# Strassen's seven block products in the first product of an MLP, on 256 columns, with w1's combinations made once and read back

## The chip, the core and the metric

The kernel runs on one core of a Trainium2 chip. The metric is the time of one execution on the device in microseconds. Five engines work side by side, each on its own queue in order: TensorE (PE; its weight loads are listed apart as PEld), VectorE (DVE), ScalarE (ACT), GpSimd (POOL) and SyncE (SP), which here only issues DMA transfers.

## What is computed

Two layers, each a linear attention and an MLP, both behind a layer norm and added to their input. Tokens S = 2048, width D = 448, 16 heads of 28, hidden width F = 1792; all in fp32.

```python
phi = lambda t: where(t > 0, t + 1, exp(t)) + 1e-6
q, k, v = heads(layernorm(x) @ wqkv)
pq, pk = phi(q), phi(k)
kv, z = einsum("bhsd,bhse->bhde", pk, v), pk.sum(s)
x = x + ((pq @ kv) / (pq @ z + 1e-6)) @ wo
h = gelu(layernorm(x) @ w1 + b1)
x = x + h @ w2 + b2
```

## The kernel before

The order of the work is written out by hand: every engine takes its instructions in the order in which the Python code issues them. fp32 accuracy is reached with fp32r products: an operand is split into a high half (a cast on ACT, "hi" or "h") and a low half (a subtraction, "lo" or "l"), and three products hi x hi, hi x lo, lo x hi are added in PSUM. The width 448 is three chunks of 128 and one of 64; the 64 rows stand twice in the fourth chunk, once with their low half, so that chunk takes two products and not three. One 128-row output with all of D takes 11 products.

A layer has two parts. `phase1` (line 733) walks over 16 tiles of 128 tokens: layer norm (statistics on DVE; the power -1/2 on POOL, line 216), the turn of the tile (DVE turns 32 x 32 squares, a transfer to DRAM and four back put them in place: `store_sq`, `spread`), splits, then k, phi(k), the running sum G of phi(k) x xn, and q. The lists `STEPS` and, after the last tile, `ORDER` (line 667) set the order; a token is one step of one tile. `ORDER` also makes the first block of four tiles ready for the MLP: `la`, `lb` (layer norm), `tu`, `st`, `sp`, `sa` (turn, store, spread) and `x0` to `x3` (the split of each tile into XH and XL).

In the first half of layer 0, the token `bg` calls `background`, which loads w1 and w2 piece by piece and splits them: a cast on ACT, a subtraction on POOL (lines 419 to 431). w1 then stays in SBUF as w1h, w1l, w1x, w2 as w2h, w2l.

The MLP walks over four blocks of 512 tokens, and in each over 14 slices of 128 hidden units. `mlp1` (line 1001) makes one slice: eleven products of 512 columns into a bank hp of PSUM, gelu on ACT into g, a cast on ACT into gh, a subtraction on DVE into gl. `mlp2` (line 1020) adds the slice to four token tiles: twelve products of 448 columns. The loop (line 1207) issues `mlp1(i + 1)` ahead of `mlp2(i)`, so TensorE has a slice's products in hand while ACT and DVE make the next gh and gl. Between the two stands `behind` (line 1097): by the tables `PLAN_0` (for block 1, while block 0 runs), `PLAN_1` and `PLAN`, with `LATER` for the second half of each, it makes the next block's attention output and its layer norm. Its tokens: `z` (POOL) and `p` (DVE: the denominator, the scaling, the turn), `sq`, `lq` (store, spread), `q` (the split), `o` (eleven products of 448 columns on TensorE, then the sum and the statistics on DVE), `n` (norm and turn), `sx`, `lx`, `x` (the split), `ld`, `g` (loads). In the last block of layer 0 the first tiles of layer 1 are prepared instead.

PSUM has eight banks: four of tag "acc" (the four token tiles of `mlp2`), two of tag "h" (hp), two of tag "m" (the output products `op`).

Of the kernel before, what the change touches and what calls it, by code (L numbers as in the profile page):

```python
# [22 lines left out]
def linear_attn_mlp_kernel(  # L23
# [22 lines left out]
    NG = D // G  # L46
    TL = D - 64
# [149 lines left out]
    w1h = wts.tile([128, 3, F], F32R, name="w1h")  # L197
    w1l = wts.tile([128, 3, F], F32R, name="w1l")
    w1x = wts.tile([128, F], F32R, name="w1x")
# [33 lines left out]
    class Block:  # L233
        def __init__(self, key):
            at = APART if key[0] == "a" else 0
            self.rows = key[0] == "m"
            self.hi = work.tile([128, 2048], F32R, name="XH", tag="XH", bufs=2)
            self.lo = work.tile([128, 2112], F32R, name="XL", tag="XL", bufs=2)[:, at:at + 2048]

        def pieces(self, t):  # L240

            if self.rows:
                return tuple(x.rearrange("p (c t n) -> p t c n", c=4, t=4)[:, t] for x in (self.hi, self.lo))
            s = slice(t * 512, (t + 1) * 512)
            return self.hi[:, s], self.lo[:, s]

        def moving(self, x, c):

            return x[:, c * 512:(c + 1) * 512]

        def still(self, x, t, c):

            return x[:, (t * 4 + c) * 128:(t * 4 + c + 1) * 128]

# [70 lines left out]
    def half_square(name, j):  # L325

        if j >= 2:
            return t512("AB"[j - 2], 2, name)
# [34 lines left out]
    def proj(name, key, j, o=None, cs=range(4), at=(3, 6, 9, 11)):  # L363
# [3 lines left out]
        if len(cs) == 4:  # L367
            w = [wkq[name, c] for c in range(3)]
            his = [(b.still(b.hi, j, c), p) for c in range(3) for p in w[c]] + [(b.still(b.hi, j, 3), wkq[name, 3])]
            los = [(b.still(b.lo, j, c), w[c][0]) for c in range(3)] + [(b.still(b.lo, j, 3), wkq[name, 3])]  # L370
# [3 lines left out]
        for c in cs:  # L374
            if c < 3:
                hi, lo = wkq[name, c]
                pe.matmul(o, b.still(b.hi, j, c), hi, start=(c == 0), stop=False)
                pe.matmul(o, b.still(b.hi, j, c), lo, start=False, stop=False)
                pe.matmul(o, b.still(b.lo, j, c), hi, start=False, stop=False)
            else:  # L380
                pe.matmul(o, b.still(b.hi, j, 3), wkq[name, 3], start=False, stop=False)
                pe.matmul(o, b.still(b.lo, j, 3), wkq[name, 3], start=False, stop=True)
# [12 lines left out]
    def bg_pieces():  # L395
        n = 0
        both = []

        def stage():
            nonlocal n  # L400
            n += 1
            if n <= LATE:
                k = (n - 1) // 2
                if k % 2 == 0 or k > 5:
                    return t512("xn", 2, "stg")[:, :D]

                if n % 2:
                    both.append(half("stg"))
                return both[-1][:, n % 2 * 512:][:, :D]
            return t448(f"W{5 + n % 2}", 1, "stg")  # L410

        for fc in range(4):
            sl = slice(fc * D, (fc + 1) * D)
            for c in range(4):
                s = stage_piece(w1[:, sl], c, sp, stage())

                def go(c=c, s=s, sl=sl):
                    if c < 3:
                        act.copy(w1h[:, c, sl], s)
                        pool.tensor_tensor(w1l[:, c, sl], s, f(w1h[:, c, sl]), op=OP.subtract)  # L420
                    else:
                        act.copy(w1x[:, sl], s)
                        pool.tensor_tensor(w1x[64:128, sl], s[64:128], f(w1x[64:128, sl]), op=OP.subtract)
                yield go
        for i in range(NF):
            s = stage()
            sp.dma_start(s, w2[i * 128:(i + 1) * 128, :])

            def go(i=i, s=s):
                act.copy(w2h[:, i], s)  # L430
                pool.tensor_tensor(w2l[:, i], s, f(w2h[:, i]), op=OP.subtract)
            yield go

    bg = bg_pieces()
    bg_wait = []

    def background(n, m=NF):

        for g in bg_wait[:m]:
            bg_wait.pop(0)()  # L440
        for _ in range(n):
            g = next(bg, None)
            if g is not None:
                bg_wait.append(g)
# [47 lines left out]
    def stage_s(l, t):  # L492
        xn = xns.pop((l, t))
        h = t512("A", 2, "xnh", F32R)
        lo = t512("B", 2, "xnl", F32R, APART)
# [81 lines left out]
    def product(name, t, c, p):  # L577
# [8 lines left out]
        pe.matmul(o, b.still(b.lo if p == "l" else b.hi, t, c), w, start=(n == 0), stop=(n == 11))  # L586
# [57 lines left out]
    def stage_g(l, t, acc, mid=lambda: None):  # L644
# [618 lines left out]
```

## Time and profile before

| what | value |
|---|---|
| median of 3 runs | 864.53 us (864.36 to 864.55) |
| profiled execution, whole | 864.72 us |
| its span, first to last instruction | 863.0 us |
| instructions | 11715 |
| TensorE's granted clock | 0.999 of full speed |
| DMA | 97.89 MB, mean 113 GB/s |

In the profile, busy time is given by engine and share of the span; matmuls overlap each other, so the steps from start to start tell what one costs and not its own duration. A group's row names line, engine, operation, output and inputs, the shape, the count, then busy us and mean ns of one, then how long the engine stood idle before these instructions and what ended that. Idle time of an engine that nobody waits for costs nothing.

### The profile page before, as it was taken

The page shows a single profiled execution, that of the slowest core. Times are in us where ns is not written, and L with a number is a line of the kernel's source. Part 1 is how long each engine was busy: PE and PEld are TensorE (multiplying, and loading weights), DVE is VectorE, ACT ScalarE, POOL GpSimd, SP SyncE. Part 2 cuts the span into 40 slices and gives each one's busy share as a digit, 9 for nine tenths or more (in the row PEclk, how much of TensorE's full clock was granted, in tenths as well). Part 3 has the DMA queues.
Part 4 walks back from the last instruction along what each step waited for, and adds up shares of the span by engine and source line. Part 5 has one row for each costly group of instructions (what it writes and reads, how often), then busy time and mean ns, then how long its engine had stood idle before and what let it go on. Part 6 is the DMA issues. An engine that isn't in the chain of part 4 may idle for free.

```text
span 863.0 us, 11715 instructions
## 1 busy us (share of the span) xinstructions
PE 857.2 (99%) x4155; PEld 768.1 (89%) x4155; DVE 493.0 (57%) x962; ACT 352.8 (41%) x635; POOL 211.6 (25%) x244
## 2 busy tenths in 40 slices
PE   9999999999999999999999999999999999999998
PEld 8999988888888888888899998988888888888887
DVE  7888586559456443236477876764664383533112
ACT  7676655323323322333356565633232233233231
POOL 3576612235013012012222343120310140140000
PEclk9999999999999999999999999999999999999999
DMA  5485647633313402051146442462332423111001
GB/s 171 150 270 180 206 108 217 191 113 121 123 61 123 140 0 98 1 182 49 49 150 188 164 130 96 146 204 81 123 113 78 140 74 111 49 49 43 1 1 43
DMA packets 68681, 97.89 MB, mean 113 GB/s; under 512 B 9488, under 2 KB 62864, under 8 KB 68624
## 3 DMA queue, kind: packets, MB, share of 16 engines
q1 hardware_dynamic: 67872, 96.76, 35.0%
q8 instruction: 32, 0.52, 0.3%
q10 hardware_dynamic: 752, 0.41, 0.2%
q14 instruction: 25, 0.20, 0.1%
HBM read 57.74 MB, written 36.18 MB: 109 GB/s over the span
## 4 chain that ended last, share of the span: by engine, by line
PE 90%; DVE 4%; DMA 3%; issue 1%; ACT 1%; POOL 1%; SPq 0%; DVEq 0%; ACTq 0%; POOLq 0%
PE hp L1011 32%; PE y L1041 10%; PE y L1040 10%; PE y L1042 10%; PE psq L372 5%; PE G L658 5%; PE psk L372 5%; PE op L949 2%; PE op L948 2%; PE op L950 2%; DMA sp<-sq_a 1%; PE op L938 1%; PE op L937 1%; PE op L939 1%; PE kvp L824 1%
## 5 line engine op out<-in xcount | busy, mean ns | idle before, releaser
L1017 DVE TENSOR_TENSOR gl<-g,gh 128x512 fp32r<-128x512 f32 x112 | 83.2, 743 | 293.0 <-ACT gh L1016 293.0
L1013 ACT ACTIVATE g<-hp,b1s 128x512 f32<-128x512 f32 x112 | 77.1, 689 | 400.8 <-PE hp L1011 400.8
L1041 PE MATMUL y<-w2l,gh 128*128 128x448 f32 x447 | 163.6, 366 | 0.0
L1040 PE MATMUL y<-w2h,gh 128*128 128x448 f32 x447 | 162.0, 362 | 0.0
L1042 PE MATMUL y<-w2h,gl 128*128 128x448 f32 x447 | 160.0, 358 | 0.0
L1011 PE MATMUL hp<-XH,w1h 128*128 128x512 f32 x336 | 130.7, 389 | 0.0
L1011 PE MATMUL hp<-XH,w1l 128*128 128x512 f32 x336 | 130.7, 389 | 0.0
L1011 PE MATMUL hp<-XL,w1h 128*128 128x512 f32 x336 | 130.1, 389 | 0.0
L216 POOL TENSOR_TENSOR brs<-bve,mhalf 128x1 f32<-128x1 f32 x55 | 34.2, 622 | 258.5 <-DVE bve L215 250.8
L1040 PEld LDWEIGHTS y<-w2h,gh 128*128 128x128 f32 x447 | 83.7, 187 | 9.4
L1041 PEld LDWEIGHTS y<-w2l,gh 128*128 128x128 f32 x447 | 83.9, 188 | 7.0
L1042 PEld LDWEIGHTS y<-w2h,gl 128*128 128x128 f32 x447 | 84.0, 188 | 5.0
L1011 PEld LDWEIGHTS hp<-XL,w1h 128*128 128x128 f32 x336 | 63.1, 188 | 13.1
L1011 PEld LDWEIGHTS hp<-XH,w1h 128*128 128x128 f32 x336 | 63.0, 187 | 10.7
L1011 PEld LDWEIGHTS hp<-XH,w1l 128*128 128x128 f32 x336 | 63.1, 188 | 9.9
L1016 ACT CAST gh<-g 128x512 fp32r<-128x512 f32 x112 | 69.6, 621 | 3.6
L372 PE MATMUL psk<-wk,XH 128*128 128x448 f32 x210 | 61.8, 364 | 0.0
L372 PE MATMUL psq<-wq,XH 128*128 128x448 f32 x196 | 57.0, 365 | 0.0
L497 POOL TENSOR_TENSOR xnl<-x,xnh 128x384 fp32r<-128x384 f32 x32 | 35.0, 1094 | 73.5 <-ACT xnh L496 60.3
L355 DVE TENSOR_TENSOR XL<-sp,XH 128x512 fp32r<-128x512 f32 x58 | 47.2, 825 | 5.7 <-ACT XH L354 5.7
L883 POOL TENSOR_TENSOR pz<-pq,zb 128x448 f32<-128x448 f32 x24 | 28.2, 1174 | 89.9 <-DVE dn L894 61.8
L658 PE MATMUL G<-kh,xnh 128*128 128x448 f32 x128 | 46.7, 367 | 0.0
(194 smaller groups left out, 1500.2 us busy)
## 6 DMA issues: line engine op xcount, KB each, us to landing
x<-in_A_x_dram SPq DMA_DIRECT2D x32, 224.0 KB, 3.9
pq_d<-eq SPq DMA_DIRECT2D x32, 224.0 KB, 2.5
pq<-pq_d SPq DMA_DIRECT2D x32, 224.0 KB, 3.6
x<-x_d SPq DMA_DIRECT2D x32, 224.0 KB, 3.9
sq_a<-sq SPq DMA_DIRECT2D x13, 512.0 KB, 2.9
sp<-sq_a SPq DMA_DIRECT2D x52, 128.0 KB, 2.9
sq_q<-sq SPq DMA_DIRECT2D x12, 512.0 KB, 2.6
sp<-sq_q SPq DMA_DIRECT2D x48, 128.0 KB, 2.8
```

What stands on the lines that cost most here:

```text
L216: pool.tensor_tensor(rs, ve, mhalf, op=OP.pow)
L355: eng.tensor_tensor(lo.rearrange("p c (i n) -> p c i n", n=32), x, f(h), op=OP.subtract)
L372: pe.matmul(o, x, p, start=(i == 0), stop=(i == 10))
L497: pool.tensor_tensor(lo[:, :TL], xn[:, :TL], f(h[:, :TL]), op=OP.subtract)
L658: pe.matmul(acc[c], w, k, start=first and c not in others[0], stop=last and c not in others[1])
L1011: pe.matmul(hp, w, r, start=(k == 0), stop=(k == len(made) - 1))
L1013: act.activation(g, hp, AF.Gelu_apprx_tanh, bias=b1s[:, i:i + 1])
L1016: act.copy(gh, g)
L1017: dve.tensor_sub(gl, g, f(gh))
L1040: pe.matmul(acc[j], gh[:, s], w2h[:, i], start=first, stop=False)
L1041: pe.matmul(acc[j], gh[:, s], w2l[:, i], start=False, stop=False)
L1042: pe.matmul(acc[j], gl[:, s], w2h[:, i], start=False, stop=stop)
```

## The change

The slices of hidden units are taken in pairs p (256 columns of w1, NP = 7 pairs), the tokens of a block in two halves of 256, the width in two halves of two chunks. The pair's product is then a product of 2 x 2 blocks, and is made with seven block products in place of eight (Winograd's form of Strassen's method). With A the tokens and B the pair of w1:

```python
SUMS = {"S1": ("A21", "A22", OP.add), "S2": ("S1", "A11", OP.subtract),
        "S3": ("A11", "A21", OP.subtract), "S4": ("A12", "S2", OP.subtract)}
PRODUCTS = {1: ("a", 0, "A11"), 5: ("a", 4, "S1"), 6: ("a", 8, "S2"), 2: ("b", 0, "A12"),
            7: ("b", 3, "S3"), 3: ("b", 7, "S4"), 4: ("b", 10, "A22")}
```

Products 1, 5, 6, 7 take six matmuls and 2, 3, 4 take five, 39 in all, each of 256 columns, where two slices took 22 of 512. In the whole kernel 2184 matmuls of 256 columns stand for 1232 of 512; the products of `mlp2`, now `quarter`, are as many as before.

*The tokens.* `token_sum` (tokens `c1` to `c4`) makes S1 to S4 on POOL, `token_piece` (`x0` to `x6`) splits A11, S1, S2, A12, S3, S4, A22: seven splits a block for four. In the first block of a layer the sums are halves of 256, eight of them, c1 c3 c2 c4; S2 needs S1, S4 needs S2.

*w1.* w1h, w1l and w1x are gone. `made_pair` makes a pair's combinations: four loads, five POOL sums of 256 columns, two transfers that swap the last chunk's halves, then casts on ACT and subtractions on POOL into two tiles of 12 and 13 x 128 columns, which are stored to DRAM; nine POOL operations of 256 and five of 128 a pair. `bg` takes a quarter of that at a time: twenty in `phase1` of layer 0 (`BG = [0] + [1, 1, 2] * 5`), eight in `ORDER`. In the MLP two pairs are in SBUF; `fetch` reads the next ones back, five of seven in each block after the first two pairs, since blocks go through the pairs in turned order. w2's splits move into layer 0's first block.

*The order in a pair.* X is a bank of tag "h", y and z are the halves of a bank of tag "m". `before` is the pair before, whose `mlp2` products are made in four quarters:

```diff
+            if 1 not in c.done:
+                c.product(1)
+            c.keep_1()
+            c.product(5)
+            c.keep_5()
+            before.rest()
+            q[0]()
+            beside(l, b, 2 * k, tr)
+            c.product(6)
+            c.keep_2()
+            fetch(held_a, fetch_a, n)
+            if 2 not in c.done:
+                c.product(2)
+            c.c11()
+            q[1]()
+            c.product(7)
+            c.c22()
+            q[2]()
+            q[3]()
+            beside(l, b, 2 * k + 1, tr)
+        c.product(3)
+        c.product(4)
+        c.c12()
...
+        def c11(self):
+            dve.tensor_tensor(self.z(), self.s1, self.z(), op=OP.add)
+            self.gelu(11, self.z())
+            self.high(11)
+            self.low(11)
...
+        def c22(self):
+            dve.tensor_tensor(self.s5, self.x(), self.s5, op=OP.add)
+            self.gelu(22, self.s5)
+            self.high(22)
+            self.low(22)
...
+        def c12(self):
+            dve.tensor_tensor(self.y(), self.s2, self.y(), op=OP.add)
...
+        def rest(self):
+            self.gelu(21, self.x())
+            self.gelu(12, self.y())
+            self.high(12)
+            self.high(21)
+            self.low(12)
+            self.low(21)
```

`keep_1`, `keep_5`, `keep_2` copy a half bank on ACT (s1, s5, s2) before the next product is added to it. `gelu` and `high` are on ACT, `low` on DVE, each 256 columns wide. A product that writes a bank waits for what last read the bank, either half of it: product 5 of a layer's first pair, the opening pair, waits for the gelu of c11, product 7 for the copy s2, product 4 for the sum of c22. The opening pair has no `before`: it makes products 1, 2, 5, 6, then products 1 of the next pair, 7, 2 of the next, 3, 4, and the last pair of a layer has its quarters in `last_step`.

*The tables.* The second half of each plan has `c` tokens and other places for `x`:

```diff
-        "x0 p0 z1",
-        "x1 p1 sq0 z2",
-        "x2 p2 z3 lq0",
-        "x3 p3 sq1",
-        "",
-        "lq1",
+        "p0 z1",
+        "c1 c3 p1 sq0 z2",
+        "x0 p2 z3 lq0",
+        "c2 x1 p3 sq1",
+        "c4 x2 x3",
+        "x4 x5 lq1",
```

The first place is DVE's queue in layer 0's first block, around the second pair. Before, from the second slice's low half to the third's (gl; dn, rd, pq0_4, sq are token p of block 1's first tile):

```order
L1017 TENSOR_TENSOR gl_1796<-g_1793,gh_1795 128x512
L894 TENSOR_REDUCE dn_1799<-pz_1736 128x16
L896 TENSOR_TENSOR dn_1799<-dn_1799,dc_1349 128x16
L898 RECIPROCAL rd_1802<-dn_1799 128x16
L905 SCALAR_TENSOR_TENSOR pq0_4_1706<-pq0_4_1706,rd_1802 128x448
L308 STREAM_TRANSPOSE sq_1805<-pq0_4_1706 128x3x4x32
L309 STREAM_TRANSPOSE sq_1805<-pq0_4_1706 128x4x32
L1017 TENSOR_TENSOR gl_1837<-g_1834,gh_1836 128x512
```

Now, from the opening pair's last sum (c12, into hy_2045) to the second pair's c22 (s5_2154; token p is of block 1's third tile):

```order
L1170 TENSOR_TENSOR hy_2045<-s2_2087,hy_2045 128x256
L1154 TENSOR_TENSOR gl_2161<-g_2158,gh_2160 128x256
L1154 TENSOR_TENSOR gl_2161<-g_2156,gh_2160 128x256
L936 TENSOR_REDUCE dn_2180<-pz_2129 128x16
L938 TENSOR_TENSOR dn_2180<-dn_2180,dc_1514 128x16
L940 RECIPROCAL rd_2183<-dn_2180 128x16
L947 SCALAR_TENSOR_TENSOR pq0_6_1977<-pq0_6_1977,rd_2183 128x448
L305 STREAM_TRANSPOSE sq_2186<-pq0_6_1977 128x3x4x32
L306 STREAM_TRANSPOSE sq_2186<-pq0_6_1977 128x4x32
L1158 TENSOR_TENSOR hy_2109<-s1_2146,hy_2109 128x256
L1154 TENSOR_TENSOR gl_2212<-g_2209,gh_2211 128x256
L1164 TENSOR_TENSOR s5_2154<-hx_2091,s5_2154 128x256
```

Before, one subtraction stood between two tokens. Now the token stands between the lows of one pair and the sums of the next, and after each sum comes the low whose gelu and cast on ACT start from that sum.

The second place is ACT's queue at the end of layer 0's attention part. Before, from the split of the first block's tiles (XH) to the first gelu (g; eq is phi(q)):

```order
L354 CAST XH_1674<-sp_1575 128x4x128 x2
L610 ACTIVATE eq_1672<-eq_1672 128x448
L354 CAST XH_1674<-sp_1645 128x4x128
L354 CAST XH_1674<-sp_1654 128x4x128
L610 ACTIVATE eq_1693<-eq_1693 128x448
L598 ACTIVATE eq_1730<-psq_1718 128x448
L599 ACTIVATE eq_1730<-eq_1730 128x448
L205 ACT_TABLE_LOAD
L205 ACTIVATE none_108<-tiny_119 128x1
L1013 ACTIVATE g_1750<-hp_1738,b1s_127 128x512
```

Now, from the split of S1 to the opening pair's first copy, s1:

```order
L1076 CAST XH_1949<-S1_1943 128x512
L1076 CAST XH_1956<-S3_1946 128x512
L1076 CAST XH_1960<-S2_1953 128x512
L653 ACTIVATE eq_1940<-eq_1940 128x448
L1076 CAST XH_1985<-S4_1964 128x512
L1080 CAST XH_1989<-sp_1886 128x8x32
L1080 CAST XH_1989<-sp_1895 128x8x32
L641 ACTIVATE eq_2007<-psq_1995 128x448
L642 ACTIVATE eq_2007<-eq_2007 128x448
L203 ACT_TABLE_LOAD
L203 ACTIVATE none_108<-tiny_119 128x1
L1129 COPY s1_2043<-hx_2036 128x256
```

The splits of S2 and S4, which wait for POOL's chain of sums, now stand ahead of the last phi(q), the table load and the copy s1.

More of the change, by code (lines that the diff above doesn't have):

```diff
@@ L392, in phi @@
         return into
[L395 to L432, printed above, removed]
@@ L701, in linear_attn_mlp_kernel @@
     PRE = 5
[L702 to L703 removed]
+    BG = [0] + [1, 1, 2] * 5
     loaded = {0: 3}
@@ L1132, in linear_attn_mlp_kernel, with last_step @@
+    def last_step():
+        while open_:
+            c = open_.pop(0)
+            c.rest()
+            for q in quarters(c):
+                q()
     table(AF.Exp)
```

429 lines of the change are left out of this document (308 added, 121 removed), and 6 rows, old and new, of the table ORDER.

## Prediction

> **What bounds the kernel now.** I read the page's busy shares first, then the waits, then the order of time on TensorE. The profiled execution took 864.72 us, 863.0 of them span; the median of the three timed runs is 864.53, so the sum below is made on 864.7 and 0.2 lies between it and the median.
>
> ```profile
> span 863.0 us, 11715 instructions
> PE 857.2 (99%) x4155; PEld 768.1 (89%) x4155; DVE 493.0 (57%) x962; ACT 352.8 (41%) x635; POOL 211.6 (25%) x244
> ```
>
> TensorE has some 6 us without work. The others wait for it, as the two largest entries of the waits show (engine and line, what it waited for, us in total, times, longest):
>
> ```profile
> ACT g L1013 <- PE hp L1011: 400.8, 110, 5.8
> DVE gl L1017 <- ACT gh L1016: 293.0, 108, 4.2
> ```
>
> So shorter TensorE work shortens the kernel, but only while no other queue makes TensorE wait. The timeline of TensorE gives its pace (start, duration, line): twelve 448-column products, then eleven of 512; then the six of 224 at the end.
>
> ```profile
> 849.53 0.36 PE L1040 MATMUL y<-w2h,gh 128*128 128x448 f32 x1
> 851.93 0.39 PE L1011 MATMUL hp<-XH,w1h 128*128 128x512 f32 x1
> 854.42 0.36 PE L1040 MATMUL y<-w2h,gh 128*128 128x448 f32 x1
> ...
> 858.62 0.26 PE L1032 MATMUL yh<-w2h,gh 128*128 128x224 f32 x1
> 859.17 0.27 PE L1034 MATMUL yh<-w2h,gl 128*128 128x224 f32 x1
> ```
>
> From start to start: 448 columns 2.40/12 = 200 ns; 512 columns 2.49/11 = 226.4 ns; 224 columns 0.55/5 = 110 ns.
>
> **TensorE's own saving.** A pair of hidden slices (256 columns of w1, one block of 512 tokens) was 22 products of 512 columns and becomes 39 of 256. There are 7 pairs, 4 blocks, 2 layers: 56. No row has 256 columns. The line through 448 and 512 (0.4125 ns a column) gives 120.8 ns; between 224 and 448 it would be 122.9; not less than the 110 of 224 columns. I take 120.8, as each of these loads new weights as the rows it comes from do. Saving: 56 x (22 x 226.4 - 39 x 120.8) = 56 x 270 ns = 15 us; ends 10.5 us (122.9) and 38.7 us (110).
>
> The row says 11 ns more than columns alone: 512 at 2.4 GHz are 213. The Trainium skill, "TensorE: Matmul & The Clock Gate", section Back-to-back issue gap, gives columns/2.4 GHz plus 2.5 ns for an isolated stream. By that rule 256 columns would take an estimated 109 ns and the saving would be 40 us; the 448 and 512 rows here stand 11 ns above it.
>
> **What the new chain costs per pair.** The rows for ACT and DVE (mean ns of one):
>
> ```profile
> L1013 ACT ACTIVATE g<-hp,b1s 128x512 f32<-128x512 f32 x112 | 77.1, 689 | 400.8 <-PE hp L1011 400.8
> L1016 ACT CAST gh<-g 128x512 fp32r<-128x512 f32 x112 | 69.6, 621 | 3.6
> L281 ACT CAST XH<-tp 128x512 fp32r<-128x512 f32 x4 | 2.3, 572 | 0.9 <-PE tp L269 0.9
> L290 ACT CAST XH<-tp 128x256 fp32r<-128x256 f32 x4 | 1.4, 368 | 0.1
> L292 DVE TENSOR_TENSOR XL<-tp,XH 128x256 fp32r<-128x256 f32 x4 | 1.6, 422 | 0.4 <-ACT XH L290 0.2
> L894 DVE TENSOR_REDUCE dn<-pz 128x16 f32<-128x448 f32 x24 | 14.6, 607 | 0.0
> L896 DVE TENSOR_TENSOR dn<-dn,dc 128x16 f32<-128x16 f32 x24 | 5.1, 214 | 0.8
> L898 DVE RECIPROCAL rd<-dn 128x16 f32<-128x16 f32 x32 | 8.1, 253 | 1.1
> L905 DVE SCALAR_TENSOR_TENSOR pq<-pq,rd 128x448 f32<-128x448 f32 x32 | 31.7, 990 | 1.0
> L308 DVE STREAM_TRANSPOSE sq<-pq 128x384 f32<-128x384 f32 x24 | 13.9, 578 | 0.8
> L309 DVE STREAM_TRANSPOSE sq<-pq 128x128 f32<-128x128 f32 x24 | 6.5, 269 | 0.0
> L969 DVE TENSOR_TENSOR x<-op,x 128x448 f32<-128x448 f32 x24 | 15.0, 624 | 4.8 <-DMA x<-x_d 1.0 <-DMA x<-in_A_x_dram 1.0
> L210 DVE BATCH_NORM_STATS2 bst<-x 128x6 f32<-128x448 f32 x55 | 34.2, 622 | 1.1 <-DMA x<-x_d 0.3
> L222 DVE BATCH_NORM_AGGREGATE bmv<-bst 128x2 f32<-128x6 f32 x55 | 10.0, 182 | 1.9
> L215 DVE TENSOR_SCALAR bve<-bmv 128x1 f32<-128x1 f32 x55 | 8.5, 154 | 1.9
> L228 DVE TENSOR_SCALAR xm<-x,bmv,brs 128x448 f32<-128x448 f32 x24 | 13.8, 575 | 0.0
> L355 DVE TENSOR_TENSOR XL<-sp,XH 128x512 fp32r<-128x512 f32 x58 | 47.2, 825 | 5.7 <-ACT XH L354 5.7
> L355 DVE TENSOR_TENSOR ql<-sp,qh 128x512 fp32r<-128x512 f32 x24 | 17.2, 716 | 0.6 <-ACT qh L354 0.6
> ```
>
> Halving the width takes 572 - 368 = 204 ns off an ACT operation: a 256-wide gelu is 0.485 us, a cast 0.417. A DVE operation of 256 is 0.42. Before, DVE did one subtraction per slice and never fed ACT. Now DVE makes the sum (c11, c22, c12), ACT's gelu and cast follow, and the very next DVE instruction (low) needs that cast. DVE takes its queue in order, so when it is behind, each sum holds it 0.42 + 0.485 + 0.417 = 1.32 us before anything else runs. A pair has three such chains and four lows: 3 x 1.32 + 4 x 0.42 = 5.65 us of DVE's queue, where TensorE needs 39 x 0.1208 + 24 x 0.2 = 9.5 us, and 2.2 more (11 x 0.2) for each output product beside it.
>
> The rest of DVE's queue comes from the plan's tokens: p = 0.607 + 0.214 + 0.253 + 0.990 + 0.578 + 0.269 = 2.91; o = 0.624 + 0.622 + 0.182 + 0.154 = 1.58; n = 0.575 + 0.578 + 0.269 = 1.42; q 0.72; x 0.83 (seven a block for four); four output adds, at o's 0.624, in pair 1 of each later block. Per pair, DVE against TensorE:
>
> First block, pairs 2 to 7: 11.5, 8.7, 13.1, 13.0, 10.2, 11.9 against 8.2 (two products already made), 11.7, 13.9, 11.7, 9.5, 9.5. Over: 3.3, 0, 0, 1.3, 0.7, 2.4 = 7.7 us.
>
> Second block: 13.3, 11.0, 12.4, 7.1, 11.5, 13.1, 9.0 against 9.5, 13.9, 13.9, 9.5, 9.5, 9.5, 9.5. Over: 3.8, 0, 0, 0, 2.0, 3.6, 0 = 9.4.
>
> Third block 0.9; fourth 0.9 in layer 0 alone. Both layers: 2 x 18.0 + 0.9 = 37 us, if TensorE waits out each excess: products 4 and 7 write a bank that c22 and the s2 copy must have read, and s2 stands in ACT's queue behind the gelu that c12 feeds. If light pairs repaid heavy ones, only the blocks' totals count: 68.4 - 64.5 + 77.4 - 75.4 = 6 us a layer, 12 in all. I take 30, nearer the upper end since there is little slack around product 7. ACT's added copies and casts lie in its 59% of free time otherwise: nothing.
>
> **The opening pair of each layer.** It has no earlier pair's products as cover. ACT and TensorE at the end of layer 0's attention half:
>
> ```profile
> 132.71 0.62 ACT L354 CAST XH<-sp 128x512 fp32r<-128x512 f32 x1 [0.17 <-DMA sp<-sq_m]
> ...
> 134.16 0.55 ACT L598 ACTIVATE eq<-psq 128x448 f32<-128x448 f32 x1 [0.34 <-PE psq L372]
> ...
> 136.63 0.20 ACT L205 ACTIVATE none<-tiny 128x1 f32<-128x1 f32 x1
> ```
>
> ```profile
> 134.12 4.99 PE hp L1011 x22
> ```
>
> ```profile
> L420 POOL TENSOR_TENSOR w1l<-stg,w1h 128x448 fp32r<-128x448 f32 x12 | 14.2, 1189 | 1.5 <-ACT w1h L419 1.3
> L498 POOL TENSOR_TENSOR xnh<-x,xnh 128x64 fp32r<-128x64 f32 x32 | 14.5, 452 | 0.0
> ```
>
> The last token tile is there at 132.7. POOL's eight half-sums of 256 (0.82 each on the line between the last two rows) follow; seven after 132.7 end at 138.5. ACT casts S4 (0.62) and A22 (2 x 0.37), then runs its old tail (134.16 to 136.83, 2.67 us, the table load in it): 142.5. Only then comes the s1 copy (0.37), c11 (0.42), gelu (0.485): 143.8. Product 5 shares product 2's bank and waits for that gelu; unhindered it would start at 134.12 + 11 x 0.1208 = 135.4. So 8.4 us, 17 in both layers (ends 3, if ACT's tail were early, and 20).
>
> **Making w1's combinations in layer 0.** Each pair costs POOL nine sums of 256 and five of 128 (0.57): 10.2 us. Five pairs lie at 17 to 100 us; these windows (us; PE, PEld, DVE, ACT, POOL busy) show POOL at 50.7 of 83:
>
> ```profile
> 17.00:50.00 33.00, 33.00 (x172) 30.59 (x171) 28.74 (x65) 22.21 (x45) 17.87 (x24) 1.00 0.52 168
> 50.00:75.00 25.00, 25.00 (x126) 23.33 (x125) 23.64 (x49) 19.77 (x38) 18.87 (x21) 1.00 0.71 228
> 75.00:100.00 25.00, 24.80 (x123) 22.82 (x123) 16.21 (x28) 16.57 (x32) 13.93 (x18) 1.00 0.65 195
> ```
>
> Without the old twenty splits (23.8) and with 51 it is 78 of 83: nearly full, with the layer norms' powers and xnl behind it, and SP's spreads behind stores that wait for POOL. I take 3 us (0 to 12). Two more pairs lie among the last tiles' norms:
>
> ```profile
> 117.44 0.55 POOL L966 TENSOR_TENSOR brs<-bst,mhalf 128x1 f32<-128x1 f32 x1 [7.67 <-ACT bst L964]
> ...
> 125.16 0.55 POOL L966 TENSOR_TENSOR brs<-bst,mhalf 128x1 f32<-128x1 f32 x1 [1.91 <-ACT bst L964]
> ```
>
> Fourteen sums (8 x 0.82 + 0.82 + 5 x 0.57 = 10.2) now stand between the first and the last of these powers: the last starts at 117.99 + 10.2 + 1.1 = 129.3, 4.1 late; I take 4 (0 to 6). Fetching w1 back is 0.79 and 0.85 MB a pair, asked for a pair (9.5 us) ahead; by the row below some 5 us: nothing, unless a spread stands behind it (up to 5).
>
> ```profile
> sq_m<-sq SPq DMA_DIRECT2D x12, 512.0 KB, 2.9
> ```
>
> **Sum.** 864.7 - 15 + 30 + 17 + 3 + 4 = 904 us.
>
> **Rivals.** (a) Light pairs repay heavy ones: 12 for 30, and the layer-0 terms between 0 and 7: 879 to 886. For it: twelve 448-column products of the pair before need nothing new. Against: c22 and s2 stand mid-pair. (b) Not slower: those 4.8 us cover every chain, ACT's tail ahead of the opening pair comes early, and waits in all stay under the 15 us saved, where it decides; with only the two 3-us openings and a few us more, some 857. Against: the first block's second pair alone asks DVE 3.3 us more than TensorE's time. (c) 256 columns at the 224 row's 110 ns: 904 - 23.7 = 880. The Trainium skill's gap rule above would be 109 ns. (d) POOL and SP stall layer 0's first half for 12 us or more and spreads come late: 925 and up. That the products don't shrink is out: 2184 of 256 columns stand for 1232 of 512.
>
> **Chances.** Forecast 0.58, (a) 0.16, (b) 0.12, (c) 0.05, (d) 0.09. 872 to 925 leaves out (b) and (d). A measurement of this kernel tells 0.2%, 1.7 us. Faster 0.11, within 0.2% 0.02 (the upper end of b), slower 0.87.
>
> **What would show it.** Right: hx and hy products at 121 ns; TensorE idle by 50 us or so, put down to ACT (gelu g, copies s2) and DVE (s5), most in blocks 1 and 2 of each layer; the third block, and the last of layer 1, shorter than before by about 2 us; an 8-us gap after the first eleven 256-column products of each layer. Wrong: TensorE over 98% busy in the loaded blocks, or the opening gap under 3 us.

## The result, and the profile after

The changed kernel takes 1006.65 us (median of four runs, 1003.35 to 1007.94) where the kernel before takes 864.54: a ratio of 1.164, with a 95% interval of 1.161 to 1.167. The forecast was 904 with a range to 925. The sign was right, and the loss was 142 us instead of 39.

The page of the changed kernel's profiled execution (1005.46 us, span 1003.7), its first two rows and, from the 40 slices, TensorE's busy share and the clock that it was granted:

```profile
span 1003.7 us, 14666 instructions
PE 892.0 (89%) x5107; PEld 822.2 (82%) x5107; DVE 590.2 (59%) x1272; ACT 478.5 (48%) x1125; POOL 296.7 (30%) x366
...
PE   9888849279888979999989999978998997999998
...
PEclk9989969679999998999999999998999999999999
```

TensorE is now without work for 111.7 us (1003.7 - 892.0; before 5.8). And it is busy for 892.0 us, more than the 857.2 of before, though its products should need less. The clock row points at a part of the reason: it falls below 9 in six slices, at or just behind slices in which TensorE's row dips (before, all forty are 9).

The waits of the whole span, three entries of the top:

```profile
DVE gl L1154 <- ACT gh L1150: 212.9, 168, 3.5
ACT g L1141 <- DVE hy L1158: 116.4, 55, 4.7
ACT s L1129 <- PE hx L1113: 95.1, 49, 4.3
```

DVE waits for ACT's cast, ACT for DVE's sum, ACT for TensorE's product: three engines take turns. Before, only gelu behind a product and the subtraction behind a cast were there, and TensorE hardly waited for either.

TensorE's own waits for this chain, from the same list (s of L1133 is the copy s2, s of L1164 the sum c22; op are the output products):

```profile
PE hx L1113 <- ACT s L1133: 28.4, 16, 4.7
...
PE hy L1113 <- ACT g L1141: 26.6, 12, 9.8
...
PE op L990 <- ACT g L1141: 7.4, 8, 1.5
...
PE hx L1113 <- DVE s L1164: 5.7, 11, 1.3
```

In their order these are product 7 behind s2, product 3 (and product 5 of the two openings) behind c11's gelu, an output product behind a gelu, and product 4 behind c22. The two openings make 18.1 of the 26.6, so 50 us are waits inside the blocks.

Where the 141 us of span lie is read from TensorE's timeline. Each column is the time from the first of the MLP's first-product matmuls in one block to that in the next (the fourth block of layer 0 includes layer 1's attention half; the last one ends with the start of the last product):

```
                first MLP   layer 0, blocks 1 to 4        layer 1, blocks 1 to 4
                product at
before            134.0      75.0  77.4  77.4  195.0       75.0  77.4  77.4  70.9
after             186.2     107.0  90.3  77.2  207.9       92.0  88.6  78.5  72.0
difference        +52.3     +32.0 +12.9  -0.2  +12.9      +17.0 +11.2  +1.1  +1.1
```

The largest piece lies ahead of the first MLP product, in layer 0's attention half. Its waits (20 to 187 us), by entries:

```profile
ACT tt L429 <- DMA low<-in_B_w_dram: 20.4, 5, 11.0
...
ACT w1b L460 <- POOL t L458: 16.6, 7, 2.9
...
PEld kvp L866 <- ACT gt L856: 14.9, 1, 14.9
...
ACT low L431 <- POOL tt L430: 12.4, 7, 5.2
```

ACT stands 49 us for the making of w1's combinations, and once TensorE stands 14.9 us for ACT. The chain of waits shows that place (start, duration, what):

```profile
131.70 0.35 SPq L462
...
138.49 3.96 DMA low<-in_B_w_dram
142.54 0.41 ACT tt L429
143.11 0.70 POOL tt L430
143.83 0.41 ACT low L431
144.24 0.44 ACT gt L856
144.72 6.12 PE kvp L866 x32
```

SP issues the next pair's loads only behind the last pair's store (L462), which waits for POOL. ACT's cast tt waits for the load, the cast low for POOL, and gt, which belongs to the attention and has nothing to do with w1, stands behind both. Before, TensorE went into this product at 104.3 us without a wait.

The opening pair of layer 1, on ACT:

```profile
672.00 0.62 ACT L1076 CAST XH<-S 128x512 fp32r<-128x512 f32 x1 [1.64 <-POOL S L1068]
...
673.88 0.71 ACT L1080 CAST XH<-sp 128x256 fp32r<-128x256 f32 x2
674.50 0.54 ACT L641 ACTIVATE eq<-psq 128x448 f32<-128x448 f32 x1
...
675.66 1.28 ACT L203 ACT_TABLE_LOAD   x1
...
677.06 0.35 ACT L1129 COPY s<-hx 128x256 f32<-128x256 f32 x1
677.91 0.47 ACT L1141 ACTIVATE g<-hy,b1s 128x256 f32<-128x256 f32 x1 [0.50 <-DVE hy L1158]
```

The queue is as forecast: S4's cast, A22's, the exponentials, the table load, and only then s1's copy and c11's gelu. Product 5 starts at 678.43, 8.55 us behind the start of product 2's last matmul at 669.88, where 0.12 is usual (forecast 8.4 late); in layer 0 it is 10.2.

What the gap does to the clock is in the windows of one microsecond around it (stretch, PE, PEld, DVE, ACT, POOL busy, granted clock, DMA):

```profile
672.00:673.00 1.00, 0.00 (x0) 0.00 (x0) 0.35 (x1) 1.00 (x2) 1.00 (x2) 0.80 0.00 0
673.00:674.00 1.00, 0.00 (x0) 0.00 (x0) 1.00 (x2) 0.73 (x3) 0.33 (x1) 0.50 0.00 0
...
682.00:683.00 1.00, 1.00 (x8) 1.00 (x7) 0.41 (x2) 0.00 (x0) 0.00 (x0) 0.58 0.68 213
683.00:684.00 1.00, 1.00 (x11) 1.00 (x10) 0.39 (x1) 0.00 (x0) 0.00 (x0) 1.00 0.63 199
```

The clock falls to 0.50 at 672.6, 2.4 us after TensorE's last product has ended, and stays there until about 682.8, 4.4 us after the work has started again. The Trainium skill, "TensorE: Matmul & The Clock Gate", Part 1 on the clock gate, describes this: half rate after an idle window of about 3.4 us, full rate after as much sustained work. The trace of this gap agrees in the two rates, and with 2.4 and 4.4 us only roughly in the times.

A pair in the loaded first block of layer 1, on DVE:

```profile
736.49 0.58 DVE L936 TENSOR_REDUCE dn<-pz 128x16 f32<-128x448 f32 x1
...
737.60 1.18 DVE L947 SCALAR_TENSOR_TENSOR pq<-pq,rd 128x448 f32<-128x448 f32 x1
...
739.51 0.40 DVE L1170 TENSOR_TENSOR hy<-s,hy 128x256 f32<-128x256 f32 x1
740.89 0.76 DVE L1154 TENSOR_TENSOR gl<-g,gh 128x256 fp32r<-128x256 f32 x2 [0.98 <-ACT gh L1150]
...
743.46 1.18 DVE L947 SCALAR_TENSOR_TENSOR pq<-pq,rd 128x448 f32<-128x448 f32 x1
...
745.38 0.40 DVE L1158 TENSOR_TENSOR hy<-s,hy 128x256 f32<-128x256 f32 x1
746.75 0.42 DVE L1154 TENSOR_TENSOR gl<-g,gh 128x256 fp32r<-128x256 f32 x1 [0.98 <-ACT gh L1150]
```

and TensorE beside it:

```profile
736.35 0.40 PE L1113 MATMUL hy<-XH,w1a 128*128 128x256 f32 x2
...
737.07 0.37 PE L1210 MATMUL y<-w2h,gh 128*128 128x448 f32 x1
...
742.00 0.50 PE L1113 MATMUL hx<-XH,w1b 128*128 128x256 f32 x2 [1.00 <-ACT s L1133]
...
746.34 0.51 PE L1113 MATMUL hy<-XH,w1b 128*128 128x256 f32 x2 [0.94 <-ACT g L1141]
```

Six products of 256 take 737.07 - 736.35 = 0.72 us, 120 ns each (forecast 120.8). c12 (L1170) and c11 (L1158) each come behind a token p of 3 us on DVE (pq, L947, is its longest operation). Product 7 (742.00) waits for the copy s2, which stands on ACT behind c12's gelu, two casts and the split of a token tile; product 3 (746.34) waits for c11's gelu.

### The profile page after: what moved, and what is told of

It reads as the page before. It is cut to its first block, busy times and chain, and to the rows that moved or that the text cites. A ratio compares the mean times of both kernels' runs of the same rounds, so it can differ in the third digit from the quotient of the medians.

```text
span 1003.7 us, 14666 instructions
## 1 busy us (share of the span) xinstructions
PE 892.0 (89%) x5107; PEld 822.2 (82%) x5107; DVE 590.2 (59%) x1272; ACT 478.5 (48%) x1125; POOL 296.7 (30%) x366
## 4 chain that ended last, share of the span: by engine, by line
PE 54%; DVE 18%; ACT 10%; POOL 6%; issue 5%; DMA 5%; SPq 2%; POOLq 0%; DVEq 0%; ACTq 0%
PE hx L1113 10%; PE hy L1113 6%; PE y L1211 5%; PE y L1210 5%; PE y L1212 5%; PE psk L369 4%; PE psq L369 4%; PE G L701 4%; ACT g L1141 3%; DVE gl L1154 2%; ACT gh L1150 2%; DVE sq L305 2%; DVE pq L947 2%; PE op L990 2%; POOL S L1068 1%
## 5 line engine op out<-in xcount | busy, mean ns | idle before, releaser
L1154 DVE TENSOR_TENSOR gl<-g,gh 128x256 fp32r<-128x256 f32 x224 | 103.5, 483 | 212.9 <-ACT gh L1150 212.9
L1212 PE MATMUL y<-w2h,gl 128*128 128x448 f32 x447 | 164.7, 369 | 0.0
L1113 PE MATMUL hx<-XH,w1b 128*128 128x256 f32 x392 | 85.5, 301 | 34.2 <-ACT s L1133 28.4
L1113 PEld LDWEIGHTS hx<-XH,w1b 128*128 128x128 f32 x392 | 68.0, 199 | 44.7 <-ACT s L1133 34.4
L1113 PE MATMUL hx<-XH,w1a 128*128 128x256 f32 x448 | 88.3, 290 | 8.8 <-ACT XH L1080 8.8
L1210 PEld LDWEIGHTS y<-w2h,gh 128*128 128x128 f32 x447 | 86.6, 194 | 5.7
L1150 ACT CAST gh<-g 128x256 fp32r<-128x256 f32 x224 | 85.4, 405 | 5.3
L1113 PEld LDWEIGHTS hx<-XH,w1a 128*128 128x128 f32 x448 | 75.9, 197 | 10.9 <-ACT XH L1080 9.1
L1113 PE MATMUL hy<-XH,w1b 128*128 128x256 f32 x336 | 74.1, 290 | 8.6 <-ACT g L1141 8.6
L1113 PEld LDWEIGHTS hy<-XH,w1b 128*128 128x128 f32 x336 | 60.3, 195 | 13.9 <-ACT g L1141 12.3
L1113 PE MATMUL hx<-XL,w1a 128*128 128x256 f32 x224 | 65.0, 290 | 0.0
L1113 PE MATMUL hx<-XL,w1b 128*128 128x256 f32 x224 | 62.7, 290 | 0.0
```

The source lines that it names most:

```text
L1113: pe.matmul(o, w, r, start=(first and k == 0), stop=(k == len(made) - 1), skip_group_check=True)
L1150: act.copy(self.h[:, s], g)
L1154: dve.tensor_sub(lo, g, f(hi))
L1210: pe.matmul(acc[j], hi[:, s], w2h[:, i], start=first, stop=False)
L1212: pe.matmul(acc[j], lo[:, s], w2h[:, i], start=False, stop=stop)
```

## The experiments

Blocks are given as in the table above; a ratio is to the kernel before. "After" is the changed kernel. Runs without a ratio were executed once. A stretch that a run leaves as it is still varies from kernel to kernel: the first MLP product starts at 184.4 to 186.9 us in runs 4, 7, 10 to 13 and 17; layer 0's first block takes 106.0 to 108.5 us in runs 1 to 3, 5, 6, 9 and 14; and layer 1's first two blocks take 91.6 to 93.2 and 87.9 to 90.4 in these and run 18. Smaller differences show nothing.

**1. No making.** made_pair's body goes; one tile per half is filled and stored once, and both fetches read it.

```
 def made_pair(p, eng):
...
+    if p == 2: sp.dma_start(w1a_d[0], f(filled(ring_a, 12 * 128)))
+    if p < 2: fetch_a(p)
```

> Leaves out the making of w1's combinations: no loads of w1, no sums, no copies between partitions, one filled tile stored once for each half and fetched for every pair, so all w1 data are constants; the 80 fetches, the token sums and all later work stay. If the making is what holds up layer 0's first half (theory), the first MLP product starts at 134 to 140 us instead of 186.2, and the time falls by about 50 to 945 to 957 us. If instead the rest of the first half (the token sums, the fetches) holds it, it starts after 170 and the time stays above 990.

Measured 955.37 us, first MLP product at 135.7. The making costs 50.6 of the 52.3 us. Token sums and fetches cost next to nothing there. The blocks stay as they were (107.4, 88.9, 77.2, 207.4; 93.2, 89.4, 78.6, 72.0): what the MLP loses has nothing to do with the making.

**2. Sums without DMAs.** `pool.memset` of top and low for the loads, no swaps, stores for pair 2 alone.

> Keeps every sum and cast of the making on POOL and ACT, leaves out its DMAs: constants instead of the loads (two fills on POOL for a pair), no copies between partitions, stores for the first pair alone. Theory of the queues (ACT, POOL and SP wait for each other's loads and stores: ACT 20.4 us and POOL 16.1 us for the loads): the first MLP product starts at 140 to 150 us, most of the 52 us come back. Rival, POOL's and ACT's load (10 us of POOL for each of seven pairs): it starts after 170 us and no more than 15 us come back.

Measured 986.37, first MLP product at 168.1: 32 of the 51 us are there without the making's loads and swaps (the fills put 7.4 us on POOL in their place). The theory had them nearly all in the DMAs; neither side's bound held. The link between ACT and POOL is still in the waits: ACT waits 16.6 us for POOL in the cast w1b and 15.9 in the cast low.

**3. and 6. DMAs without sums**, twice, with the extra fetches at the end and then spread.

> The other half: keeps the loads, the copies between partitions and the stores of the making on SP's queue, leaves out its sums and casts (one tile of each half, filled once, is stored for every pair; four extra fetches at the end). Theory of the queues: with nothing to wait for, the DMAs alone cost 0 to 8 us, the first MLP product starts at 134 to 142 us. Rival, traffic: 52 us of delay come from the bytes and from SP's issues, it starts after 155 us.

> The DMAs of the making without its sums, once more, with the four extra fetches spread over the first and sixth pair instead of standing together behind the last (there they held the last spreads by 15.8 us). Theory: 135 to 143 us for the first MLP product, so that DMAs alone cost under 8 us. Rival, traffic and SP's issues: 150 us or later.

Measured 975.35 and 980.66, first MLP product at 156.5 and 161.6. Neither is clean. In the first, the four extra fetches stand ahead of the last spreads, and TensorE waits 15.8 us at the end; in the second SP waited for a store before it could fetch the same rows back, and TensorE stood 11.1 us at 48.4. If these waits are taken off whole, 140.7 and 150.5 are left; so DMAs alone cost an estimated 5 to 15 us, and these two runs say no more.

**5. Sums unlinked.** The same sums and casts on constants, into scratch.

```
+    def sums(n, cols=256, rows=slice(0, 128)): eng.tensor_tensor(y[rows, ...], x[rows, ...], x[rows, ...], op=OP.subtract)
+    def copies(n, cols=256): act.copy(z[...], x[...])
```

> Sums and casts of the making with the same engines, shapes, number and places, but all on constants and into scratch tiles, so that no cast waits for a POOL sum and no sum for a cast; no DMAs of the making except as in the run without any making; w1's data are constants. The linked sums started the first MLP product at 168.1 us, no making at 135.7. Theory of the link (ACT stands in its queue until POOL has made what it casts, 16.6 and 15.9 us in the waits of that run, and the attention work behind it comes late): 136 to 148 us. Rival, the load of POOL and ACT: 158 us or later.

Measured 979.22, first MLP product at 161.2, 25.5 us later than in run 1. TensorE stands 6.9 us behind the filling of the constants (seven wide casts on ACT at 39 to 45 us); run 1 has the same casts and no such pause, so how much of it belongs to the filling is not known. So some 20 to 25 us come with POOL's and ACT's plain load: the rival, not the link, holds the larger part.

**9. Loads a stage earlier.**

```
+        if p != 1:
+            raw_loads((p + 1) % NP)
         sp.dma_start(w1a_d[p], f(w1a[p]))
```

> The loads of w1 for the next pair are issued one stage earlier, ahead of this pair's two stores on SP's queue; all else of the making is as in the change. Theory (SP sends a pair's loads only behind the store that waits for POOL's last sum of the pair before; ACT waits 20.4 us and POOL 16.1 us for them): most of the 18 us between the linked sums alone (168.1) and the full change (186.2) come back, the first MLP product starts at 168 to 178 us and the time falls by 8 to 18 us. Rival (the bytes, or the copies between partitions): within 4 us of the change.

Measured 987.87 (ratio 1.143, 1.140 to 1.147), first MLP product at 172.7. ACT's wait for the load of low is gone from the list (its wait for POOL in the cast low went from 12.4 to 17.0), and the 14.9 us in front of kvp have become 4.0. SP's order cost 13.6 us.

**14. Copies on POOL.**

```
-        act.copy(low[:, 1], f(tt))
+        pool.tensor_copy(low[:, 1], f(tt))
...
-        act.copy(gb[:, 12], t4[:, 1])
+        pool.tensor_copy(gb[:, 12], t4[:, 1])
```

> The change with the two copies of the making for which ACT waits on POOL in mid-pair (low from tt, and the last part of w1b; 16.6 and 12.4 us of waiting in the change) done by POOL itself, behind its own sums: some 1.3 us more of POOL for a pair, no round trip. Theory of the link: ACT's attention work no longer stands behind them, the first MLP product starts at 172 to 180 us instead of 186.2, the time falls by 6 to 14 us. Rival (POOL's load is what costs): later than 186 and slower.

Measured 1004.91 (1.162, 1.160 to 1.164), first MLP product at 187.0: no gain. The wait moved to what stood behind it (20 to 170 us):

```profile
ACT tt L429 <- DMA low<-in_B_w_dram: 37.0, 6, 14.2
```

against 20.4 before the edit. With the loads early as well (run 15), the first MLP product comes at 164.7, 8.0 earlier than with the loads early alone; the other edit of run 15 that touches the first half leaves it at 186.8 (run 8). The link costs 8 us, but only once the loads no longer hide it.

**4. Subtractions on POOL.** `pool.tensor_tensor(lo, g, f(hi), op=OP.subtract)` for `dve.tensor_sub(lo, g, f(hi))`.

> The subtraction gl = g - gh (224 of 256 columns) goes from DVE to POOL, so that DVE no longer stands still for ACT's cast (212.9 us of waiting in 168 pieces). Theory (the chain sum, gelu, cast, subtraction in DVE's queue is what TensorE waits for in the loaded blocks): the first three blocks of layer 1 lose most of their 22 us of TensorE idle beyond the opening, layer 0's likewise, and the time falls by 30 to 50 us to 955 to 975. Rival (tokens' work as such, or POOL then stands in for DVE with its powers and token sums behind the subtractions): the time moves by less than 10 us either way.

Measured 985.17 (1.140, 1.138 to 1.142), 21 us off; between the two sides. It helps the last block of layer 0 (207.9 to 200.0) and the second blocks (90.3 and 88.6 to 84.4 and 83.4), and does nothing for the first of layer 1 (92.0 to 91.6).

**7. Subtractions later, still on DVE.** Out of c11, c22 and rest; 11 and 22 at the step's end, 12 and 21 behind its first tokens.

> The four subtractions gl = g - gh of a pair stay on DVE but are queued behind the tokens and beside the next work (11 and 22 at the end of the step, 12 and 21 after the first tokens of the next), so DVE no longer stands at a subtraction while ACT does gelu and cast; nothing is added to POOL. Theory of the chain in DVE's queue: the waits of DVE for gh fall from 213 us to under 80, layer 1's first three blocks from 92.0, 88.6 and 78.5 us to about 84, 80 and 77, and the whole kernel by 25 to 45 us to 960 to 982. Rival (DVE's plain load of tokens, not its standing): less than 10 us.

Measured 1005.08 (1.161, 1.158 to 1.164): nothing in all. DVE's wait for gh falls from 212.9 to 36.3 us, but others have taken its place over the whole span:

```profile
ACT g L1141 <- DVE hy L1158: 133.8, 55, 6.2
ACT s L1129 <- PE hx L1113: 127.5, 52, 4.1
...
PEld y L1208 <- DVE gl L1154: 50.3, 40, 3.4
```

The sum c11 (hy) is as late as before, since the tokens are still ahead of it, and the second product now waits for gl, TensorE itself for 35.5 us. The fourth block of layer 0 gained 9 us, the first blocks lost 8 and 3. So this place for the subtractions gains nothing; that DVE's standing costs nothing is not shown, since the edit brought a wait of its own.

**10. Sums ahead of the tokens.**

```
             q[0]()
-            beside(l, b, 2 * k, tr)
             c.product(6)
...
             c.c11()
+            beside(l, b, 2 * k, tr)
             q[1]()
...
-            beside(l, b, 2 * k + 1, tr)
         c.product(3)
         c.product(4)
         c.c12()
+        if not fresh:
+            beside(l, b, 2 * k + 1, tr)
```

> In every step but a layer's first, DVE gets the sums ahead of the tokens: products 6 and 2 and the sum c11 come before the step's first tokens, products 3 and 4 and c12 before its second. Nothing is added or left out. Theory now (TensorE waits for a sum that stands behind 3 to 5 us of tokens in DVE's queue, and DVE is nearly full in the first two blocks, so that taking its standing away alone could not help): blocks 0 and 1 of layer 1 go from 92.0 and 88.6 us to 84 to 88 and 78 to 84, the time falls by 15 to 35 us. Rival (DVE's sum of work alone sets it): within 6 us.

Measured 979.96 (1.133, 1.130 to 1.136), 27 us off. Layer 1's second block goes from 88.6 to 83.6, as expected; the first only to 90.2, less than expected. TensorE's waits tell why: that for s2 falls from 28.4 to 3.7 us and that for c11's gelu to the 17.8 of the openings, but a step's first tokens now stand ahead of c22, and product 4 waits 29.8 us for that sum instead of 5.7. The call `beside` moves the tokens of all engines, TensorE's output products and ACT's splits among them, so the run shows what their place costs, not which queue alone does it.

**11. and 12. Both orders, and POOL with it.**

> Sums ahead of the tokens as in the run before, and the subtractions gl behind the next sum or the tokens' start, so that DVE stands less. Theory: another 5 to 15 us below the run with the sums first alone. Rival (DVE's work, not its standing): within 4 us of it.

> Sums ahead of the tokens, and the subtractions gl on POOL. DVE has both less work and no standing. Theory: the lowest of the three, 8 to 20 us below the run with the sums first alone; layer 1's first two blocks near 82 and 79 us. Rival (POOL is late with them): above it.

Measured 975.32 (1.127, 1.123 to 1.131) and 980.64 (1.134, 1.130 to 1.137). The 5 us between run 10 and run 11 are not clear of the noise, as the two intervals overlap: a cost of DVE's standing, once the sums are early, is not shown. POOL in DVE's place gives nothing beyond that order (layer 1's first block 90.5: POOL waits for gh in its turn, 98.7 us in all).

**13. No subtractions.** Run 11 with `self.g[q] = hi, hi`: gh stands in gl's place.

> The run with sums first and subtractions late, with the subtractions gl left out (gh stands in their place in the third product, so the output lacks that correction); TensorE's work is the same, DVE has 4 x 0.4 us less for a pair. Theory (in blocks 0 and 1 DVE's queue is as long as TensorE's): block 0 of layer 1 falls from 89.4 to 80 to 85 us, block 1 from 82.3 to 77 to 80. Rival (what is left there is the pair's own chain of copy, sum and gelu, or ACT, or POOL): both within 2 us.

Measured 969.21; layer 1's first two blocks 86.6 and 81.0 where run 11 has 89.4 and 82.3. The first is outside both sides, the second on the rival's and within the spread. So the subtractions, their work and their waits, are a part of what is left in the first block, 2.8 us, not all of it. TensorE's wait for c22, behind the tokens, is as long as in run 11: 20.2 us over the kernel, and 20.5 there.

**8. The opening.**

```
-"... c1 c3 x1 c2 x4 x2 c4 Qe Qj Qs pre x5 x6 Qa Qi Qj Qs "
+"... c1 c3 c2 c4 Qe Qj Qs pre Qa Qi Qj Qs "
...
             c.c11()
+            for j in (1, 4, 2, 5, 6):
+                token_piece(l, b, j)
             c.product(5)
```

> At each layer's opening the casts of S1, S2, S3, S4 and A22 are queued behind the last of the attention's exponentials, the table load, s1's copy and c11's gelu, not ahead of them. Theory (ACT's queue ahead of s1 makes the gap of 10.2 us in layer 0 and 8.6 in layer 1): the gaps shrink to 3 to 6 us, and the time falls by 6 to 12 us to 994 to 1001. Rival (the POOL sums are what is late): the gap only moves to the next product that needs S1 or S2, and the time stays within 3 us.

Measured 994.55 (1.151, 1.148 to 1.153), 12 us off. The first pair of layer 1 takes 11.6 us instead of 15.1, that of layer 0 15.3 instead of 20.4. The gap ahead of product 5 goes from 8.55 to 3.91 and from 10.2 to 5.2, as expected: the casts in ACT's queue were the cause of half of it. What is left are the exponentials, the table load, s1's copy and c11's gelu.

**17. The opening's gap filled** with products nobody reads.

```
             c.product(2)
+            idle = bank("acc", 4, "idle")
+            for _ in range(28):
+                pe.matmul(idle, xs_[l, b, "A11"][0][:, :128], xs_[l, b, "A11"][0], start=True, stop=True)
             c.c11()
```

> 28 products of 512 columns into an unused bank (6.3 us, results unused) are put into the opening's gap of each layer, behind product 2; the gap itself stays. In the change the granted clock falls to 0.50 in that gap and the 256-column products after it run at some 213 ns for 2.5 us, where 120 is usual. Theory (the gap is paid twice: TensorE's clock comes back only after some us of work): with the gap filled the clock stays at 1.00, the first pair of layer 1 takes 13 to 14 us instead of 15.1, and the kernel gains 2 to 5 us. Rival (what follows a gap is as late as the chain is, clock or not): the first pair stays within 0.4 us.

Measured 999.44 (1.155, 1.152 to 1.157), but the first pair of layer 1 only went from 15.1 to 14.6, between the two sides, and most of the 7 us lie at other places. In the profiles 1.8 us lie ahead of the first filling, where the two kernels are the same. The filling ended too early: product 5 starts 2.16 us behind the start of the last filling product, TensorE is idle for 1.77 of them, and the windows show the clock at half rate all the same:

```profile
674.00:675.00 1.00, 0.17 (x1) 0.17 (x2) 0.27 (x1) 0.67 (x2) 0.66 (x1) 1.00 0.86 260
675.00:676.00 1.00, 1.00 (x8) 1.00 (x9) 0.75 (x2) 0.37 (x2) 0.48 (x1) 0.84 1.01 324
...
678.00:679.00 1.00, 1.00 (x6) 1.00 (x6) 0.77 (x2) 0.00 (x0) 0.00 (x0) 0.50 0.74 240
679.00:680.00 1.00, 1.00 (x10) 1.00 (x9) 0.43 (x1) 0.00 (x0) 0.00 (x0) 0.95 0.61 188
```

So this run did not isolate what the clock costs.

**18. w2 without its loads**, a constant tile split 14 times.

> Leaves out the loads of w2: one constant tile is split 14 times in its place (casts on ACT and subtractions on POOL stay), so that nothing of the splits waits for a DMA. Block 0 of layer 0 takes 107.0 us, that of layer 1, which has no splits, 92.0. Theory (ACT stands at a split whose load is late, 6.2 us in the waits, with s2's copy and the gelu of the pair behind it): block 0 of layer 0 falls to 96 to 101 us. Rival (the splits' work itself on ACT and POOL): it stays at 104 or more.

Measured 996.00; layer 0's first block 102.0 instead of 107.0. A third of its 15 us over layer 1's first block is ACT standing for w2's loads; neither side's number. The trace agrees: product 7's wait for s2, which stands on ACT behind these splits, is 12.6 us in layer 0's first block and 3.2 in layer 1's, and 8.6 in this run. The rest was not taken apart.

**15. and 16. Together, and with the making for nothing.**

> All the mended queues in one: w1's loads a stage earlier, the two copies on POOL, the opening's casts behind c11, the sums ahead of the tokens and the subtractions late. If their gains add (14, 6 to 14, 11 and 31 us) 935 to 950 us; still far from 864.5, since POOL's and ACT's load in the first half (25 us) and DVE's in the blocks are still there.

> What the seven products can give if w1's combinations cost nothing: no making as in the first run (constants for w1's data), with the opening's casts behind c11, sums first and subtractions late. The gains add to 905 to 920 us. If the blocks' products alone were worth their 15 us, it would come below 864.

Measured 943.75 (1.093, 1.091 to 1.095) and 911.86. The gains add up to about what was expected, and no run is faster than the kernel before. Without any making and with the better orders, the blocks are 96.0, 81.7, 76.6, 201.2 and 85.3, 80.8, 76.6, 72.1: only the third block of each layer beats the eight products, by 0.8 us. TensorE still waits 18.0 us for c22 in run 16, so these orders need not be the best.

## Why the prediction was wrong, step by step

**TensorE's own saving: right.** 120.0 ns for 256 columns (120.8 taken), so 56 x (22 x 226.4 - 39 x 120.0) = 16.8 us for the 15 forecast. Rival (c), 110 ns, is out. (The 512 row stands 13 ns above 213, not 11.) Some 6 us of it go back in a way that I had not seen: the second product's matmuls, untouched by the change, start every 203, 208 and 203 ns (medians by line, from all their start-to-start times) where it was 199, 205 and 196; 14 ns for three, and there are 448 such threes. The cause is open.

**The opening pair: right in layer 1**, 8.55 us for 8.4, by the queue that was named; 10.2 in layer 0. Run 8 shows it for the casts, with half of the gap gone.

**The fetches at nothing: nothing speaks against it.** No wait for a fetched tile is in the changed kernel's list, and run 1, which keeps all fetches, starts the MLP at 135.7. With the better orders (runs 10 to 13, 15 and 16) TensorE waits 2.3 to 4.7 us for w1b.

**Layer 0's first half: this step failed.** "78 of 83: nearly full [...] I take 3 us (0 to 12)", with 4 more for the last tile. It was 52.3, of which 50.6 are the making. What failed is the reading of a busy share as a price: I added POOL's operations to its free time and found that they fit. In sum they do: they took 9.1 us a pair for the 10.2 forecast, and POOL is busy for only 49.0 of those 83 us (17 to 100) in the changed kernel. But POOL, ACT and SP each serve the attention and the making in one order, and a tile's power or cast that finds itself behind a pair's sums is late by them, however much time is free later. The runs put some 20 to 25 of the 50.6 us on POOL's and ACT's load (run 5), 13.6 on SP's loads behind the stores (run 9) and 8 on the casts of ACT that wait for POOL (run 15 against 9). The fourth rival had this mechanism, at 925 and up and a chance of 0.09; it alone makes a third of the loss.

**The blocks' chain: mechanism half right, size wrong.** I took 30 us for both layers. Layer 1 went up by 30.4; with 8.4 us saved on products, 8.4 lost in the opening and about 3 on the slower second products, 27 are left for the chain, where 15 stood. In layer 0 (57.6 up, 10 of it opening) it is 53. Of these 80 us TensorE waits 50, by its list above; some 22 of the rest are slow products (below). I had priced what DVE is short of, pair by pair, and let TensorE wait for the excess alone. But the sums stand behind the tokens: even where DVE's total would fit, TensorE waits out the token ahead of c11 or c12. Run 10 shows that the place of the tokens costs this: with the order changed and no operation less, 27 us come back, and what stays is in good part the third sum, c22, which the new order puts behind them. What the wait that I had named, DVE at the subtraction, is worth by itself is open: taking the subtractions off DVE gave 21 us (run 4), queueing them later nothing in all (run 7), and behind run 10's order neither gave a clear gain (runs 11 and 12). In layer 0, block 4 lost some 13 us, where 0.9 was forecast, all of it in its products (70.7 us before, 83.8 now; layer 1's attention half takes 124 in both): ACT, DVE and POOL also prepare layer 1's weights and first tiles there. For 47 us, from 471 to 518, the chain of waits in the changed kernel does not touch TensorE; in part:

```profile
471.59 4.30 DMA stg<-in_A_wqkv_dram
475.90 1.53 ACT wk L138 x3
...
478.11 1.61 DVE wk L148
479.75 0.44 DVE hy L1158
...
500.21 0.55 DVE bst L208
...
501.23 0.56 POOL brs L214
501.82 0.52 DVE x L504
...
503.13 0.33 DVE hy L1158
```

A cast that waits for a load stands in ACT's queue, and c11 (hy, L1158) comes behind it on both engines. At 500 it is a tile's layer norm: DVE makes the statistics, stands for POOL's power, scales and turns, and c11 comes behind. No run separates the two; run 7 gets 9 of the 13 us back. In layer 0's block 1, w2's splits do the like, 5 us by run 18. So ACT's added work, which I had put at nothing because it fitted ACT's free time, was the same misreading as in the first half.

**Third blocks, and the last of layer 1, shorter by 2 us: wrong.** -0.2, +1.1 and +1.1: the slower second products and a residue of the chain.

**A term that was missing: the clock.** Start-to-start times between 1.3 and 2.2 times the usual for their width make 37 us beyond the usual in the changed kernel (312 of them) and 5.5 in the kernel before (44): 200 of the 312, with 24.0 of the 37 us, start while the granted clock is 0.50. It fits TensorE's busy time, which rose by 35 us while its work fell. I priced a wait at its length; a wait of TensorE of two or three us or more can be followed by slow products. How much of the 142 us this makes was not isolated (run 17).

## What to carry to other kernels

Work put into the free time of an engine that is in a critical loop is priced by what stands behind each piece in its queue, not by the share of time that is free: here 78 of 83 us seemed to fit, and cost 20 us or more. A change that takes work off the bounding engine and makes it depend on three others within each step needs slack in every step; put the operations that the bounding engine waits for ahead of the filling, not behind it, and all of them: with two of three sums moved ahead, TensorE waited for the third. Here the seven products save 17 us, and in every order that was tried they lose more than that, even if w1's combinations cost nothing.

## What the runs showed of the hardware

TensorE's granted clock in the changed kernel is 0.50 in 13 stretches, 99 us in all, of which TensorE is busy for 61; in the kernel before it is 1.00 up to the last 1.5 us. Each stretch lasts a whole multiple of 3.41 us (27.3 the longest), and each begins during a pause of TensorE or within 1.4 us behind one. Of the changed kernel's pauses of over 1.8 us all but one (1.94) have such a stretch, among them seven of 1.88 to 3.37 us; in run 17 a pause of 1.77 us brought 3.41 us of it. A pause of this length does not always do so: in run 8, four of 2.47 to 3.09 us left the clock at 1.00. The page of the Trainium skill named above speaks of an idle window of about 3.4 us; here shorter pauses were enough, and the measurement decides.

Removing one wait of a queue can move the whole of it to the next: ACT's wait for w1's loads went from 20.4 to 37.0 us when its waits for POOL were taken away, with the same total time.
